# Attention and two MLPs on one core: the first MLP in six tiles of 512 tokens instead of eight of 384

## The chip, the core and the metric

The kernel runs on one core of a Trainium2 chip. The core has a matrix engine (TensorE, PE in the profile, with its weight loads as PEld), a vector engine (VectorE, DVE), an activation engine (ScalarE, ACT), GpSimd (POOL), and SyncE (SP), which here only issues DMA transfers. Each engine runs its own instructions in their order and waits on semaphores for the others. The metric is the device time of one execution in microseconds (us), lower is better.

## What is computed

Three layers in a row, over 4 x 768 = 3072 tokens of 8 heads x 64 = 512 features, in fp32:

```python
for c in range(S // 32):                       # attention in chunks of 32 queries
    k_full = concat([mem_k, k[max(0, 32*c - 16) : 32*c + 40]])      # 8 memory keys and a window
    a = exp(s - max(s));  a = a / (sum(a) + 1e-9)                   # s = q_c @ k_full.T / 8
    out[32*c : 32*c + 32] = a @ v_full
h = x @ w_in;  g = where(h > 0, h, exp(min(h, 0)) - 1);  x = g @ w_out      # first MLP, 512-2048-512
h = x @ w_in2; g = s * relu(h)**2 + b;                   y = g @ w_out2     # second MLP, 512-2048-512
```

## The kernel before

**Attention.** The tokens are cut into 24 units of 128 (U). For a unit u there are three steps: S (step_S: 64 small matmuls of scores on PE, then softmax on DVE, with the exp on ACT; units at the edge of a batch, u % 6 in (0, 5), have a mask added first), P (step_P: the probabilities are transposed into the tile pt), and V (values: 64 small matmuls with pt, then to_x). For the first NU0 = 6 units P is four PE transposes and a copy of their result; for the others it is 16 transposes of 32x32 blocks on DVE, and V of u and S of u+1 share one step (step_VS), V first.

**First MLP.** Each fp32 operand is split into a high and a low part in fp32r, and a product is three matmuls (mm3, L326 to L328). A tile t is a run of units; sizes = [3] * 8, so 384 tokens. The 2048 hidden features are 16 columns c of 128. A slot (t, c) is h1(t, c), 12 matmuls into psH, with the ELU behind it (L350, L351 on ACT, L352 on DVE gives g; gh on ACT and gl on DVE, L184, are its two parts), and out1 of the slot two before it, 12 matmuls into the four accumulators acc. The slots run (0, 0..5), (1, 0..15), (0, 6..15), (2, 0..15), ... (7, 0..15). Since tile 0 is interrupted, its accumulators go out to part_dram and are added back later (L376); at the end of a tile the accumulators are evacuated (big) and stored to y_dram.

**Where attention runs.** Units of tile 0 go before the first slot. Those of tile 1 are spread over slots (0, 0..5), those of tile 2 over (0, 6..15), the others over tiles 2 to TATT - 1 = 4, by a count of steps (beside). From tile 2 on a unit's output goes through DRAM: xs to x_dram (to_x), and load_x reads a whole tile back four slots before its end, copies it to xh on ACT and takes xl on DVE. In slots of tiles 0 and 1 the weights are converted and split (split_w); after the attention, from (5, 0) on, prepare makes the sums of the second MLP's weights and stores them to s_dram.

**Second MLP.** A Strassen-like scheme with seven products (ORDER), in three passes of 1024 tokens; pieces of the weights come from s_dram by a ring of 12 buffers (ws), and load_blocks makes the seven token blocks xc of a pass. Its matmuls have 512 columns.

**What sets the order.** Instructions go out in the order of the program text as a scheduler has moved them (it weighs estimated times and the priorities of the code), each engine in its own queue. Pools give the buffers; before, the first 8 weight columns (NFREE) lay in one pool on the right and the rest in one on the left, whose memory was given back as a whole when MLP one neared its end.

Of the kernel before, what the change touches and what calls it, by code (L numbers as in the profile page):

```python
# [20 lines left out]
P = 128  # L21
# [6 lines left out]
NP = H // 2  # L28
NU0 = 6
HF = 6  # L30
TATT = 5
NFREE = 8
MICRO = 8
HN, NT2 = 512, 3
ORDER = (1, 2, 6, 5, 7, 3, 4)
BANK = {1: 1, 2: 2, 6: 1, 5: 5, 7: 1, 3: 5, 4: 1}
# [17 lines left out]
def tile_attention_then_two_mlps(ctx, tc, q_in, k_in, v_in, w1, w2, s_in, b_in, out):  # L54
# [22 lines left out]
    def engine(step):  # L77
# [4 lines left out]

    sizes = [3] * 8
    assert sum(sizes) == NU
# [6 lines left out]
    mctx = ExitStack()  # L91
    early = [ExitStack(), ExitStack()]
    wps = [early[0].enter_context(tc.tile_pool(name="wpa", bufs=1, side="right")),
           mctx.enter_context(tc.tile_pool(name="wpb", bufs=1))]
    wst = mctx.enter_context(tc.tile_pool(name="wst", bufs=3))
    one = mctx.enter_context(tc.tile_pool(name="one", bufs=1))
    xp = mctx.enter_context(tc.tile_pool(name="xp", bufs=1))
    gp = mctx.enter_context(tc.tile_pool(name="gp", bufs=4))
# [23 lines left out]
    def load_w(w, c, i):  # L122

        r = wps[c >= NFREE].tile([P, DM, 2], I32, tag=f"w{i}_{c}", name=f"raw{i}_{c}")
        nc.sync.dma_start(out=r, in_=w[c, i].bitcast(I32).rearrange("p (n z) -> p n z", z=2))
        return r
# [15 lines left out]
    def split_w(c, i, raw):  # L142

        t = wst.tile([P, DM], I32, tag="t", name="t")
        yield from to_f32(raw, t)
        nm = "io"[i]
        parts = wps[c >= NFREE].tile([P, 2, DM], F32R, tag=f"w{i}_{c}", name=f"w{i}_{c}")
        hi, lo = parts[:, 0], parts[:, 1]
        nc.scalar.activation(out=hi, in_=f(t), func=AF.Copy)
        sub(lo, f(t), hi)  # L150
        W[nm, c], WT[nm, c] = (hi, lo), parts
        yield
# [211 lines left out]
    def put_out(t, c, n):  # L364
# [6 lines left out]
        if c == NF - 1 or c == HF - 1 and split:  # L371
            for m, acc in enumerate(ACC[t]):
                with tc.high_priority(400):
                    if c == NF - 1 and split:
                        o = PART.pop(m)
                        nc.vector.tensor_tensor(out=o, in0=o, in1=acc[:, :n], op=ALU.add)  # L376
                    else:
                        o = big_tile(n, t >= TATT and m > 0 or m == 3 and t >= 2)
                        if m % 2:
                            nc.vector.tensor_copy(o, acc[:, :n])  # L380
                        else:
                            nc.scalar.activation(out=o, in_=acc[:, :n], func=AF.Copy)
                store = nc.scalar if t == NTILE1 - 1 else nc.sync
                store.dma_start(out=y_dram[:, m, t0:t0 + n] if c == NF - 1 else part_dram[:, m, :n], in_=o)
# [138 lines left out]
    pieces = pieces * NT2  # L523
    ws, used = [], [0]

    def load_pieces(n):

        while len(ws) < min(n, len(pieces)):
            lay, ii, jj = pieces[len(ws)]
            w = p2["wsp"].tile([P, 2, 2 * P], F32R, tag="ws", name="ws")  # L530
            nc.sync.dma_start(out=f(w), in_=s_dram[lay, ii, :, PIECE[jj]])
            ws.append(w)
# [8 lines left out]
    XC = {}  # L541

    def load_blocks(t):

        t0 = t * 2 * HN
        xc = XC[t] = {j: p2["xcp"].tile([P, 2, 2, HN], F32R, tag=f"xc{j}", name=f"xc{j}") for j in ORDER}
        b12 = p2["yrp"].tile([P, 2, HN], F32, tag="yr", name="b12")
        b11, b21, b22 = (f(xc[j][:, 1]) for j in (1, 2, 3))
        for o, r, z in ((b11, 0, 0), (b12, 0, 1), (b22, 1, 1), (b21, 1, 0)):
            nc.sync.dma_start(out=o, in_=y_dram[:, 2 * r:2 * r + 2, t0 + z * HN:t0 + (z + 1) * HN])  # L550
        if t == 0:
            load_pieces(12)
        t3, t2, t4 = (p2["yrp"].tile([P, 2, HN], F32, tag="yr", name=nm) for nm in ("t3", "t2", "t4"))
        for o, x, y in ((t3, b22, b12), (b12, b12, b11), (t2, b22, b12), (t4, b21, t2)):
# [3 lines left out]
        for j in ORDER:  # L558
            nc.scalar.activation(out=xc[j][:, 0], in_=src[j], func=AF.Copy)
            sub(xc[j][:, 1], src[j], xc[j][:, 0])  # L560
            yield

    def open_second():

        for nm, k, c in (("xcp", 1, ctx), ("wsp", 12, ctx), ("yrp", 4, early[1])):
            p2[nm] = c.enter_context(tc.tile_pool(name=nm, bufs=k, side="right", reuse_waits="tile"))
        p2["blocks"] = load_blocks(0)

    def mlp1_step(t, c):
# [6 lines left out]
        elif t == 0:  # L576
            a0, total, k, ks = ready[1], ready[2] - ready[1], min(c - HF, NF - HF - 4), NF - HF - 3
        elif 1 < t < TATT:
            a0, total, k, ks = ready[2], len(steps) - ready[2], NF * (t - 2) + c, NF * (TATT - 2)

# [4 lines left out]
        elif t == 1:  # L585
            n0 = 8 * HF + 12
            wt = [(w1, max(n0 + (MICRO * NF - n0) * (2 * c + z) // 28, MICRO * (c + z)), 4) for z in (1, 2)]
        if c == 0 and t == TATT:
            actx.close()
            op.append(mctx.enter_context(tc.tile_pool(name="op2", bufs=2)))  # L590
            p2["prep"] = early[1].enter_context(tc.tile_pool(name="prep", bufs=2, side="right", reuse_waits="tile"))
            p2["steps"] = prepare_all()
            nc.sync.dma_start(out=s_sb, in_=s_in.to_broadcast([P, 1]))
            nc.sync.dma_start(out=b_sb, in_=b_in.to_broadcast([P, 1]))
        if t < 2:
            weights_to(w1, MICRO * (c + 1), 4)
        if t == NTILE1 - 1 and c == NFREE + 2:
            early[1].close()
            early[0].close()
            open_second()  # L600
# [5 lines left out]
        prepared(t, 2 * c + 2)  # L606
        if t == NTILE1 - 1 and c >= NFREE + 2:
            for _ in range(3):
                next(p2["blocks"], None)
# [4 lines left out]
    def prepared(t, n):  # L614

        want = min(NPREP * (2 * NF * (t - TATT) + n) // (2 * NF * (NTILE1 - TATT) - 2 * (NF - NFREE)), NPREP)
        while t >= TATT and p2["n"] < want:
            next(p2["steps"])
# [12 lines left out]
    for slot in seq[-2:]:  # L631
# [5 lines left out]

    early[1].close()
    g2p, evp, outp, p2["yrp"] = (
        ctx.enter_context(tc.tile_pool(name=nm, bufs=k, reuse_waits="tile"))  # L640
        for nm, k in (("g2p", 4), ("evp", 5), ("outp", 4), ("yrp2", 4)))
    ghp = ctx.enter_context(tc.tile_pool(name="ghp", bufs=3, side="right", reuse_waits="tile"))
    psp = ctx.enter_context(tc.tile_pool(name="psp", bufs=8, space=PSUM, reuse_waits="tile"))
# [15 lines left out]
    def first_layer(t, i, g):  # L659

        xc, ii, acc = XC[t], i % 2, {}
        for j in ORDER:
# [4 lines left out]
            for k in range(2):  # L667
                mm3(o, (w[:, 0], w[:, 1]), (xc[j][:, 0], xc[j][:, 1]), lambda a: a[:, k * P:(k + 1) * P],
                    lambda a: a[:, k], j in (1, 2, 5) and k == 0, k == 1, j not in (1, 2, 5))
# [25 lines left out]
    def second_layer(t, gs, beside):  # L695

        keep, acc = {}, {}
        for j in ORDER:
# [4 lines left out]
            for q, g in enumerate(gs):  # L703
                gl, gh = (ghp.tile([P, 2, HN], F32R, tag=nm, name=nm) for nm in ("g2l", "g2h"))
                nc.scalar.activation(out=gh, in_=g[:, block], func=AF.Copy)  # L705
# [98 lines left out]
```

## Time and profile before

| | us |
|---|---|
| median of 3 runs (1089.6 to 1096.9) | 1091.55 |
| the profiled execution | 1094.46 |
| its span, from first to last instruction | 1092.7 |
| first matmul of the first MLP | 28.67 |
| first matmul of the second MLP | 623.38 |
| PE busy in the span | 1072.1 |
| DVE busy | 783.6 |
| ACT busy | 592.1 |

The span is what the trace shows; the run's time has 1.76 us around it. Starts are in us from the span's start. A matmul's duration in the trace overlaps that of the next one, so its price is the distance of starts. "PEclk" is the clock that TensorE was granted, as a share of its full 2.4 GHz. "Idle before" is the time in which an engine had nothing to do in front of a row, with the instruction that ended it.

### The profile page before, as it was taken

To read this page: it belongs to the slowest core of one execution; us is meant where nothing else is said; L and a number is where in the kernel's file an instruction comes from. 1 tells how busy PE (TensorE), PEld (TensorE's weight loads), DVE (VectorE), ACT (ScalarE), POOL (GpSimd) and SP (SyncE) were. 2 spreads that over 40 slices of the span, in tenths; PEclk is the share of its full clock that TensorE was granted. 3 is DMA by queue.
4 is the path that set the end of the run, shared out by engine and by line. 5 is a ranking of instruction groups with operands and counts; after the bars stand their busy time and mean duration, and the time that the engine had idled before them with its cause. 6 is when DMAs were issued, how large, how long until landed. Compare 5 with 4: busy or idle time off the path is not lost.

```text
span 1092.7 us, 20633 instructions
## 1 busy us (share of the span) xinstructions
PE 1072.1 (98%) x8206; PEld 966.0 (88%) x8206; DVE 783.6 (72%) x1299; ACT 592.1 (54%) x939; POOL 0.7 (0%) x6
## 2 busy tenths in 40 slices
PE   7999999999999999999999999999999999999998
PEld 5889999999999999999999987788888788888887
DVE  6899846778678777998884655697356696365854
ACT  4888444334434446787784455754355644255542
POOL 0000000000000000000000000000000000000000
PEclk7899999999999999999999999999999999999999
DMA  8955032433524315898886266777766777766673
GB/s 307 373 221 220 1 109 88 153 102 105 174 81 145 125 40 173 319 335 298 331 326 236 90 187 191 244 210 231 230 191 185 231 214 225 212 197 191 200 204 127
DMA packets 98113, 213.70 MB, mean 196 GB/s; under 512 B 9952, under 2 KB 27360, under 8 KB 95968
## 3 DMA queue, kind: packets, MB, share of 16 engines
q1 hardware_dynamic: 97440, 211.59, 59.4%
q8 instruction: 65, 1.06, 0.4%
q10 hardware_dynamic: 576, 0.79, 0.2%
q14 instruction: 32, 0.26, 0.1%
HBM read 164.89 MB, written 47.45 MB: 194 GB/s over the span
## 4 chain that ended last, share of the span: by engine, by line
PE 82%; DVE 8%; DMA 5%; ACT 3%; issue 1%; SPq 0%; ACTq 0%; DVEq 0%
PE psH L326 14%; PE psH L328 13%; PE psH L327 13%; PE psL L327 7%; PE acc L326 6%; PE psL L328 6%; PE acc L327 6%; PE acc L328 6%; PE psL L326 6%; DVE pt L258 2%; DMA xc<-y_dram 2%; DMA xl<-x_dram 1%; DMA x_dram<-xs 1%; PE psVS L278 1%; PE psVS L219 1%
## 5 line engine op out<-in xcount | busy, mean ns | idle before, releaser
L326 PE MATMUL psH<-xh,w 128*128 128x384 f32 x512 | 175.4, 343 | 2.6 <-ACT pt L180 1.1
L326 PE MATMUL acc<-gh,w 128*128 128x384 f32 x512 | 173.0, 339 | 0.9 <-DVE big L376 0.8
L328 PE MATMUL psH<-xh,w 128*128 128x384 f32 x512 | 173.6, 339 | 0.0
L327 PE MATMUL psH<-xl,w 128*128 128x384 f32 x512 | 173.2, 338 | 0.2 <-DVE xl L184 0.2
L327 PE MATMUL acc<-gl,w 128*128 128x384 f32 x512 | 171.9, 336 | 0.0
L328 PE MATMUL acc<-gh,w 128*128 128x384 f32 x512 | 171.9, 336 | 0.0
L705 ACT ACTIVATE g2h<-g 128x1024 fp32r<-128x1024 f32 x84 | 89.2, 1062 | 89.9 <-PE psL L328 89.6
L327 PE MATMUL psL<-g2l,ws 128*128 128x512 f32 x336 | 131.0, 390 | 1.6 <-DVE g2l L184 1.6
L326 PE MATMUL psH<-xc,ws 128*128 128x512 f32 x336 | 131.8, 397 | 0.6 <-ACT p L656 0.6
L328 PE MATMUL psH<-xc,ws 128*128 128x512 f32 x336 | 131.1, 390 | 0.0
L326 PE MATMUL psL<-g2h,ws 128*128 128x512 f32 x336 | 130.4, 389 | 0.6 <-ACT g2h L705 0.6
L327 PE MATMUL psH<-xc,ws 128*128 128x512 f32 x336 | 130.9, 390 | 0.0
L328 PE MATMUL psL<-g2h,ws 128*128 128x512 f32 x336 | 130.7, 389 | 0.0
L184 DVE TENSOR_TENSOR g2l<-g,g2h 128x1024 fp32r<-128x1024 f32 x84 | 102.2, 1222 | 39.5 <-ACT g2h L705 39.2
L350 ACT ACTIVATE g<-psH 128x384 f32<-128x384 f32 x128 | 62.5, 488 | 113.1 <-PE psH L328 67.0
L180 ACT ACTIVATE gh<-g 128x384 fp32r<-128x384 f32 x128 | 66.9, 522 | 86.8 <-DVE g L352 85.6
L352 DVE SCALAR_TENSOR_TENSOR g<-g,psH 128x384 f32<-128x384 f32 x128 | 70.5, 551 | 49.3 <-ACT g L351 48.4
L326 PEld LDWEIGHTS psH<-xh,w 128*128 128x128 f32 x512 | 97.0, 189 | 5.2 <-ACT pt L180 1.4
L326 PEld LDWEIGHTS acc<-gh,w 128*128 128x128 f32 x512 | 96.6, 189 | 2.4 <-DVE big L376 1.1
L327 PEld LDWEIGHTS psH<-xl,w 128*128 128x128 f32 x512 | 97.1, 190 | 0.5 <-DVE xl L184 0.4
L328 PEld LDWEIGHTS psH<-xh,w 128*128 128x128 f32 x512 | 97.2, 190 | 0.2
L327 PEld LDWEIGHTS acc<-gl,w 128*128 128x128 f32 x512 | 96.2, 188 | 0.3 <-DVE gl L184 0.2
(97 smaller groups left out, 1668.1 us busy)
## 6 DMA issues: line engine op xcount, KB each, us to landing
ws<-s_dram SPq DMA_DIRECT2D x336, 256.0 KB, 2.9
raw<-w SPq DMA_DIRECT2D x64, 512.0 KB, 5.4
s_dram<-right SPq DMA_DIRECT2D x16, 1024.0 KB, 4.5
kb<-k SPq DMA_DIRECT2D x24, 512.0 KB, 5.6
v<-v SPq DMA_DIRECT2D x24, 512.0 KB, 4.3
s_dram<-left SPq DMA_DIRECT2D x16, 768.0 KB, 3.6
q<-q SPq DMA_DIRECT2D x24, 256.0 KB, 5.5
out<-r SPq DMA_DIRECT2D x24, 256.0 KB, 3.5
```

The source lines that it names most:

```text
L180: return nc.scalar.activation(out=hi, in_=src, func=AF.Copy)
L184: return nc.vector.tensor_tensor(out=lo, in0=src, in1=f(hi), op=ALU.subtract)
L219: mm = nc.tensor.matmul(ps[o, z, r * NCK:(r + 1) * NCK], q[rows, r * U + c * CH:r * U + (c + 1) * CH], kb[rows, r, c * NCK:(c + 1) * NCK], ...
L258: nc.vector.transpose(out=pt[k * CH:(k + 1) * CH, :, rows], in_=sm[rows, :, z, n0:n0 + CH])
L278: nc.tensor.matmul(ps[r % 2 * D:(r % 2 + 1) * D, z, o:o + CH], v[rows, (r * NC + c) * D:(r * NC + c + 1) * D], pt[rows, r, cs], start=True ...
L326: nc.tensor.matmul(o, sa(a[0]), sb(b[0]), start=first, stop=False, skip_group_check=again)
L327: nc.tensor.matmul(o, sa(a[0]), sb(b[1]), start=False, stop=False, skip_group_check=again)
L328: return nc.tensor.matmul(o, sa(a[1]), sb(b[0]), start=False, stop=last, skip_group_check=again)
L350: nc.scalar.activation(out=g[:, :n], in_=ps[:, :n], func=AF.Relu, scale=-1.0)
L352: nc.vector.scalar_tensor_tensor(out=g[:, :n], in0=g[:, :n], scalar=-1.0, in1=ps[:, :n], op0=ALU.add, op1=ALU.max)
L705: nc.scalar.activation(out=gh, in_=g[:, block], func=AF.Copy)
```

## The change

The first MLP takes tiles of four units, 512 tokens, six of them. Units 0 to 3 (tile 0) go before the first slot and units 4 to 7 beside slots (0, 0..5); NU0 = 8, so the first eight units are transposed on PE. The other attention units, from 12 on, are spread over the slots from (2, 0) to ATT_END = (3, 8) instead of over three tiles, and prepare starts at (3, 8). The weights of the first layer lie in one pool (wpi), with the x tiles on the same side; those of the second in another (wpo). The second MLP takes its buffers over from these pools one by one, under the same tags: the blocks xc and the ring of pieces from weight columns w0_c (two pieces to a buffer) and from an x tile, the first blocks yr from w1_0 to w1_3, and the parts of g for its second layer from the other x tile. The order of the operations within the second MLP is not edited.

```diff
-NU0 = 6
+NU0 = 8
-TATT = 5
-NFREE = 8
+ATT_END = (3, 8)
+NBLOCK = 10
...
-    sizes = [3] * 8
+    sizes = [4] * 6
...
-    early = [ExitStack(), ExitStack()]
-    wps = [early[0].enter_context(tc.tile_pool(name="wpa", bufs=1, side="right")),
-           mctx.enter_context(tc.tile_pool(name="wpb", bufs=1))]
+    wps = [ctx.enter_context(tc.tile_pool(name="wpi", bufs=1, side="right")),
+           mctx.enter_context(tc.tile_pool(name="wpo", bufs=1))]
-    xp = mctx.enter_context(tc.tile_pool(name="xp", bufs=1))
+    xp = ctx.enter_context(tc.tile_pool(name="xp", bufs=1, side="right"))
...
-        r = wps[c >= NFREE].tile([P, DM, 2], I32, tag=f"w{i}_{c}", name=f"raw{i}_{c}")
+        r = wps[i].tile([P, DM, 2], I32, tag=f"w{i}_{c}", name=f"raw{i}_{c}")
...
+            n = len(ws) % 12
+            if len(ws) < 12 and n % 2 == 0:
+                p2["ws"] += [high(10 + n // 2)]
+            w = p2["ws"][n // 2].rearrange("p z (j n) -> p (z j) n", j=2)[:, 2 * (n % 2):2 * (n % 2) + 2]
...
+    def high(c):
+        return wps[0].tile([P, 2, HN], F32R, tag=f"w0_{c}", name=f"hi{c}")
...
-        elif 1 < t < TATT:
-            a0, total, k, ks = ready[2], len(steps) - ready[2], NF * (t - 2) + c, NF * (TATT - 2)
+        elif t > 1 and (t, c) < ATT_END:
+            a0, total, k, ks = ready[2], len(steps) - ready[2], NF * (t - 2) + c, NF * (ATT_END[0] - 2) + ATT_END[1]
...
-        if t == NTILE1 - 1 and c == NFREE + 2:
-            early[1].close()
-            early[0].close()
+        if t == NTILE1 - 1 and c == NBLOCK:
             open_second()
...
+        begin = 2 * (NF * ATT_END[0] + ATT_END[1])
+        want = min(NPREP * (2 * NF * t + n - begin) // (2 * NF * (NTILE1 - 1) + 2 * NBLOCK - 2 - begin), NPREP)
```

How PE's instructions stand at the start, before (psS scores, psP transposes, psV values, psH the first layer-one matmuls; the scheduler's counts of small matmuls are those of its own rows):

```order
L219 MATMUL psS<-kb,q 32x64 x15
L251 MATMUL psP<-ident,sm_103 128x128 x4
L278 MATMUL psV<-pt,v 64x32 x32
L219 MATMUL psS<-kb,q 32x64 x32
L326 MATMUL psH<-xh,w_0_382 128x384
```

And now, from the same scores on:

```order
L218 MATMUL psS<-kb,q 32x64 x15
L250 MATMUL psP<-ident,sm_103 128x128 x4
L277 MATMUL psV<-pt,v 64x32 x32
L218 MATMUL psS<-kb,q 32x64 x32
L250 MATMUL psP<-ident,sm_104 128x128 x4
L277 MATMUL psV<-pt,v 64x32 x32
L218 MATMUL psS<-kb,q 32x64 x32
L325 MATMUL psH<-xh,w_0_433 128x512
```

The transposes, the values and the following scores of unit 3 have moved ahead of the first psH matmul.

On DVE, before, the end of unit 15's probabilities (multiply by the reciprocal sums, 16 transposes into pt) and what stands until the softmax of unit 16 begins (nmx), with the xl of an x tile:

```order
L237 TENSOR_TENSOR sm_103<-sm_103,rs 128x2x4x64
L258 STREAM_TRANSPOSE pt<-sm_103 32x4x32
L352 SCALAR_TENSOR_TENSOR g<-g,psH 128x384
L258 STREAM_TRANSPOSE pt<-sm_103 32x4x32 x4
L184 TENSOR_TENSOR gl<-g,gh 128x384
L258 STREAM_TRANSPOSE pt<-sm_103 32x4x32 x11
L184 TENSOR_TENSOR xl<-xl,xh 128x1536
L352 SCALAR_TENSOR_TENSOR g<-g,psH 128x384
L184 TENSOR_TENSOR gl<-g,gh 128x384
L352 SCALAR_TENSOR_TENSOR g<-g,psH 128x384
L184 TENSOR_TENSOR gl<-g,gh 128x384
L231 TENSOR_REDUCE nmx<-psVS 128x8
```

Now the like place, the end of unit 16's and the begin of unit 17's, which has a mask (cmask):

```order
L236 TENSOR_TENSOR sm_103<-sm_103,rs 128x2x4x64
L257 STREAM_TRANSPOSE pt<-sm_103 32x4x32 x11
L351 SCALAR_TENSOR_TENSOR g<-g,psH 128x512
L257 STREAM_TRANSPOSE pt<-sm_103 32x4x32 x4
L183 TENSOR_TENSOR gl<-g,gh 128x512
L257 STREAM_TRANSPOSE pt<-sm_103 32x4x32
L183 TENSOR_TENSOR xl<-xl,xh 128x2048
L351 SCALAR_TENSOR_TENSOR g<-g,psH 128x512
L227 TENSOR_TENSOR sm_104<-psVS,cmask_93 128x2x4x64
L183 TENSOR_TENSOR gl<-g,gh 128x512
L230 TENSOR_REDUCE nmx<-sm_104 128x8
```

Between xl and the next softmax stand one g and one gl now, not two of each; on PE, 48 matmuls stand between the scores of one unit and the values of the next from unit 13 on (60 at the turn of a tile), where 72 or 84 stood before.

## Rows read from the trace of the kernel before

**Rows 1.** The page: span.

```profile
span 1092.7 us, 20633 instructions
PE 1072.1 (98%) x8206; PEld 966.0 (88%) x8206; DVE 783.6 (72%) x1299; ACT 592.1 (54%) x939; POOL 0.7 (0%) x6
```

**Rows 2.** Windows by stage: stretch, length, busy time of each engine, PEclk, DMA share.

```profile
0.00:28.67 28.67, 21.47 (x546) 16.71 (x546) 18.06 (x38) 12.35 (x20) 0.70 (x6) 0.78 0.84 311
28.67:96.86 68.19, 63.76 (x730) 57.25 (x725) 65.08 (x128) 61.57 (x120) 0.00 (x0) 0.94 0.81 309
96.86:623.38 526.52, 524.21 (x4921) 516.33 (x4921) 403.21 (x851) 287.01 (x538) 0.00 (x0) 1.00 0.48 166
623.38:1092.70 469.32, 462.67 (x2017) 375.70 (x2016) 297.27 (x284) 231.20 (x264) 0.00 (x0) 1.00 0.70 205
```

**Rows 3.** Timeline of PE: first matmuls of slots (5, 0) and (7, 15).

```profile
419.04 0.44 PE L326 MATMUL psH<-xh,w 128*128 128x384 f32 x1
...
615.07 0.33 PE L326 MATMUL psH<-xh,w 128*128 128x384 f32 x1
```

**Rows 4.** Timeline of PE: two matmuls of the second MLP, 202 apart.

```profile
880.18 0.39 PE L326 MATMUL psL<-g2h,ws 128*128 128x512 f32 x1
...
925.97 0.39 PE L327 MATMUL psL<-g2l,ws 128*128 128x512 f32 x1
```

**Rows 5.** Timeline of PE, then DVE: start, duration, what; values, scores, first psH.

```profile
16.87 1.94 PE L278 MATMUL psV<-pt,v 64*64 64x32 f32 x64
...
22.76 1.11 PE L251 MATMUL psP<-ident,sm 128*128 128x128 f32 x4
24.62 1.72 PE L278 MATMUL psV<-pt,v 64*64 64x32 f32 x56 [0.75 <-ACT pt L180]
27.19 0.44 PE L278 MATMUL psV<-pt,v 64*64 64x32 f32 x8 [0.85 <-issue]
27.56 1.18 PE L219 MATMUL psS<-kb,q 64*32 64x64 f32 x64
28.67 0.69 PE L326 MATMUL psH<-xh,w 128*128 128x384 f32 x1
...
30.32 0.68 DVE L237 TENSOR_TENSOR sm<-sm,rs 128x512 f32<-128x512 f32 x1
```

**Rows 6.** Timeline of PE at unit 6's values, then windows behind them.

```profile
74.74 0.30 PE L278 MATMUL psVS<-pt,v 64*64 64x32 f32 x2 [0.93 <-DVE pt L258]
75.40 0.78 PE L278 MATMUL psVS<-pt,v 64*64 64x32 f32 x38 [0.36 <-DVE pt L258]
...
77.00:81.00 4.00, 4.00 (x16) 3.87 (x14) 4.00 (x9) 3.47 (x8) 0.00 (x0) 0.57 0.97 334
```

**Rows 7.** Timeline of PE and DVE: unit 15, scores, first and last transposes, values.

```profile
275.25 0.86 PE L219 MATMUL psVS<-kb,q 64*32 64x64 f32 x64
...
284.74 2.58 DVE L258 STREAM_TRANSPOSE pt<-sm 32x128 f32<-32x128 f32 x8
...
290.82 0.38 PE L278 MATMUL psVS<-pt,v 64*64 64x32 f32 x12
```

**Rows 8.** Timeline of PE: values of unit 16.

```profile
305.40 0.55 PE L278 MATMUL psVS<-pt,v 64*64 64x32 f32 x24
306.43 0.30 PE L278 MATMUL psVS<-pt,v 64*64 64x32 f32 x2 [0.48 <-DVE pt L258]
307.09 0.78 PE L278 MATMUL psVS<-pt,v 64*64 64x32 f32 x38 [0.36 <-DVE pt L258]
```

**Rows 9.** Groups by line and form: busy time, mean ns, idle before; 384 and 512 columns.

```profile
L352 DVE SCALAR_TENSOR_TENSOR g<-g,psH 128x384 f32<-128x384 f32 x128 | 70.5, 551 | 49.3 <-ACT g L351 48.4
L649 DVE TENSOR_TENSOR g<-m,psH 128x512 f32<-128x512 f32 x24 | 16.5, 687 | 24.1 <-PE psH L328 18.2 <-ACT m L656 5.6
```

**Rows 10.** Timeline: x tile 2 on its way through DRAM.

```profile
168.12 0.60 ACT L180 ACTIVATE xs<-psVS 128x512 f32<-128x512 f32 x1 [0.51 <-PE psVS L219]
...
180.64 1.76 DVE L184 TENSOR_TENSOR xl<-xl,xh 128x1536 fp32r<-128x1536 f32 x1 [1.00 <-ACT xh L302]
```

**Rows 11.** The page: DMA issues, us from issue to landing.

```profile
ws<-s_dram SPq DMA_DIRECT2D x336, 256.0 KB, 2.9
```

## What the change does to the time

> **What bounds the kernel now.** I read the span first: PE is busy 98% of 1092.7 us [rows 1]. The stage windows then say where it is not: 7.2 us before the first layer-one matmul at 28.67, 4.4 us up to 96.86, only 2.3 us from there to the second MLP at 623.38, 6.7 us in the second MLP [rows 2]. So the time is a count of matmuls times their spacing, plus the attention's own small matmuls, plus few waits. The profiled execution took 1094.46 us, 1.76 more than its span; the median is 0.27% under it. My sum goes by the span; the result is scaled by 1091.55/1094.46.
>
> **Spacing of a matmul.** From 419.04 to 615.07 there is no idle, and 47 slots of 24 matmuls, 1128, start in 196.03 us: 173.8 ns for 384 columns [rows 3]. In the second MLP 202 spacings of 512-column matmuls fill 880.18 to 925.97: 226.7 ns [rows 4]. So a third more columns costs 30.4% more, as if about 14.8 ns of each matmul were fixed.
>
> **The change, part by part.**
>
> *Fewer, wider matmuls.* MLP one has 128 slots of 24 = 3072 matmuls before and 96 of 24 = 2304 after: 3072 x 0.1738 = 533.9 us against 2304 x 0.22667 = 522.2 us: **-11.7**, if the fp32r matmul of MLP one keeps the pace of that of MLP two, whose form is the same but for the tiles' names. By a price per column (0.1738 x 512/384 = 0.2317) it is 533.9 us again: 0. I take -11.7, since a 512-column row is nearest to a 512-column matmul. The Trainium skill ("TensorE: Matmul & The Clock Gate", section "Back-to-back issue gap") gives a warm gap of about N/2.4 + 2.5 ns, 162.5 and 215.8 ns here: by it the gain is an estimated 2.0 us and not 11.7. The trace shows 11 ns more than that at either width, so the measurement decides.
>
> *Longer start.* A first tile of four units puts P3, V3 and S5 of unit 3 ahead of the first layer-one matmul. Before, DVE ends unit 3's softmax at 30.32 + 0.68 = 31.0 [rows 5]. Behind it come four transposes at half clock (1.1, as those of unit 2 at 22.76), the pt copy's wait (0.75, as at 24.62), V3 (1.7) and most of S5 (0.8): 35.3 against 28.67, **+6.6**. Bounds: V ends of units 0 and 2 lie 8.8 us apart, 4.4 a unit; with V2's extra 0.85 us of issue, 7.5.
>
> *The stretch from there to slot (1,6).* 264 matmuls: 45.9 us of 68.19 before, 59.8 after. Of the other 22.3 us before, about 10.7 are PE work of units 3 to 6, 4.4 idle, 1.8 the half clock at its head (twelve matmuls 0.32 us apart). After, PE work is that of units 4 to 7, four times 2.85 = 11.4. Unit 6 was turned by DVE's 32x32 transposes, and PE waited 0.93 + 0.36 us inside its V; from 77 to 81 us the clock then stood at 0.57, which costs 4 x 0.43 = 1.7 [rows 6]. Both go, as units 6 and 7 are now transposed on PE. Of the rest I take 6.2 us: the floor is 59.8 + 11.4 + 1.8 = 73.0, and with all 22.3 it is 82.2. DVE (65.1 us busy of 68.2) and ACT (61.6) get some 7% more nominal work in the longer stretch, so they do not pass PE. I say 77.5, **+9.3**.
>
> *From slot (1,6) to the second MLP.* Before, 526.52 us: 2808 matmuls (115 slots and 48) 488.0, 17 units with V and S the other 38.5, that is 2.27 each, of which 2.75 us in all were waits, so 2.1 each without. After: 83 slots of 5.440 and 48 matmuls, 462.4; 16 units 33.6; together 496.0.
>
> *The waits in V.* Here the change bites. For each of these units DVE does, behind the scores S on PE, maximum, subtract, (ACT's exp), sum, reciprocal, multiply and 16 transposes of 0.30, and V of the unit waits for the last. Unit 15 is typical: S ends at 275.25 + 0.86 = 276.11, the transposes at 284.74 + 2.58 = 287.32: 11.2 us with one g and one gl between; PE came to V at 290.82, having 84 matmuls [rows 7]. Unit 16, with 72, waited 1.33 us in V (two idles, 0.48 and 0.36, and pieces) [rows 8]. After, the attention has 24 slots for twelve units from (2,0) on, and the order has 48 matmuls between S and the next V: 10.9 us, some 11.4 until V's last matmuls need the last transposes. The chain becomes 11.2 + 2 x 0.13 (g and gl at 0.69 and not 0.55 [rows 9]) = 11.5. So:
> - plain units (15, 16, 19, 20, 22): 0.2 each, 1.0; unit 14 0.4;
> - 9, 10, 11 and 13, with evacuations and partial adds of the accumulators, a mask, or a V that stands 12 matmuls earlier: 1.6, 1.9, 1.35, 1.9;
> - 23, masked: 0.9; units 8, 12 and 18 have 60 matmuls or more: 0;
> - 17 and 21, where xl of the next x tile stands in DVE ahead of the softmax. Before, that chain took 14.3 us from xs at 168.12 to the end of xl at 180.64 + 1.76 [rows 10]; for 2048 columns ACT takes 0.6 and DVE 0.55 more and the transfer is a third larger: 16.6 to 17.8. S of the next unit ends 13.0 us on, so DVE starts its softmax some 4 us late: 5.1 (with mask, g and gl) and 3.8.
>
> Sum 17.9 against 2.75 before. 496.0 + 17.9 = 513.9: **-12.6**. Bounds: 2.75 (they hide as before) and 30 (each of the seven waits above 0.9 us brings a half clock at 1.7 us, as from 77 to 81; unit 16's 1.33 brought none).
>
> *x staging.* X2 is ready 17.8 us behind V11 at the latest, PE has 19 us of work until h1(2,0). Without that cover: up to 4 us.
>
> *Weights in parts, buffers taken over singly.* In the second MLP the instructions keep their order. Its first twelve pieces wait each for h1 of the last six slots and land 2.9 us after issue [rows 11]; 36 matmuls (8.2 us) lie between the last h1 and the first use. 0, with +/-1.5 for the block loads. Without that cover, 2.9 us once. prepare runs in 34 slots of 5.44 = 185 us instead of 40 of 4.17 = 167: no wait on PE before, none after.
>
> Sum: +6.6 + 9.3 - 12.6 = **+3.3 us** on 1092.7, i.e. 1096.0; with 1.76 and scaled 1095.
>
> **Rivals.** About 1% (10.9 us) is what a measurement tells from no change: faster is under 1080.6, slower over 1102.5.
> 1. *The waits hide.* If the evacuations, the partial adds and xl run in gaps of DVE and not, as I have them, ahead of a softmax, and the plain chains stay 0.2 us under unit 15's, the waits stay at 2.75 and the sum is 3.3 - 15.1 = -11.8: 1080. For it: DVE is busy 77% of the long stretch [rows 2], and of 17 units only four waited before. Against: their gap was 72 to 84 matmuls, 12.5 to 14.6 us, and DVE does its queue in order.
> 2. *Waits and clock.* As forecast, but each long wait also drops the clock to its lower level (1.2 GHz) for some us: +12, 1107. It decides from a wait of about 1 us on. For it: after 0.93 us at 74.7 the clock fell. Against: after the pair of unit 16 it did not; that wait at 74.7 stood in a stretch with other idles.
> 3. *No gain per matmul.* If the spacing goes by columns (231.6 ns) the term of -11.7 is 0: 1107. For it: the weights and moving operands now lie apart, which no row here prices. Against: the two spacings differ by less than the columns do [rows 3, 4]. By the formula of the Trainium skill ("TensorE: Matmul & The Clock Gate", "Back-to-back issue gap") the estimate is 1104; no row here bears it out at either width.
>
> **How the numbers follow.** Forecast 0.54 (1083 to 1102 by its own bounds: start -2 to +1, stretch +/-4.5, waits 10 to 22), rival 1 0.20, rival 2 0.17, rival 3 0.09. Predicted is the forecast, 1095. Rival 1 stands on the edge of "faster": with the start and the stretch at their low ends it is under it; I give it 0.16 faster and 0.04 within. Rivals 2 and 3 are mostly slower: 0.21 of their 0.26, 0.05 within. So faster 0.16, same 0.63, slower 0.21. The range 1080 to 1107 leaves out about 0.2.
>
> **What would show it.** 226.7 ns between 512-column matmuls of psH and acc; h1(0,0) at 35 us (under 33 or over 37: wrong); slot (1,6) at 112.8; the second MLP's first matmul at about 626.7; idle of PE before psVS released by DVE's pt, 15 to 18 us in sum, largest at units 17 and 21, with xl in front of the softmax; the granted clock at 1.00 after them (else rival 2). I am wrong if the V waits sum to under 6 us, if the second MLP changes by over 2 us, or if the first tiles are bounded by DVE or DMA, for which the share is 0.84 at the start.

## The result and the profile after

| | before | after |
|---|---|---|
| median of 7 runs each (us) | 1092.85 | 1099.35 |
| profiled execution, span (us) | 1092.7 | 1097.1 |
| first matmul of the first MLP | 28.67 | 35.29 |
| first matmul of slot (1, 6) | 96.86 | 109.96 |
| first matmul of the second MLP | 623.38 | 628.58 |

The ratio is 1.007, with an interval of 1.0052 to 1.0087: 0.7% slower, inside the 1% that the prediction called "no change", and inside its range. The span grew by 4.4 us where 3.3 were forecast.

The windows by stage of the changed kernel (stretch, length, busy time of PE, PEld, DVE, ACT, POOL, then granted clock, DMA share, GB/s) answer to [rows 2]:

```profile
0.00:35.29 35.29, 25.50 (x678) 20.08 (x678) 24.68 (x52) 16.34 (x27) 0.70 (x6) 0.72 0.86 322
35.29:109.96 74.67, 73.41 (x734) 58.05 (x730) 70.87 (x132) 67.38 (x125) 0.00 (x0) 0.97 0.76 276
109.96:628.58 518.62, 509.74 (x4026) 414.32 (x4025) 375.15 (x733) 262.98 (x426) 0.00 (x0) 0.99 0.47 163
628.58:1097.10 468.52, 462.54 (x2017) 375.63 (x2015) 297.38 (x284) 231.06 (x264) 0.00 (x0) 1.00 0.71 206
```

Against before the stages changed by +6.6, +6.5, -7.9 and -0.8 us. The long third stage is where the gain was to be: PE now idles 8.9 us in it, not 2.3.

**The spacing.** The timeline of PE of the changed kernel, first matmuls of slots (4, 0) and (5, 14), answers to [rows 3]:

```profile
446.92 0.39 PE L325 MATMUL psH<-xh,w 128*128 128x512 f32 x1
...
612.12 0.39 PE L325 MATMUL psH<-xh,w 128*128 128x512 f32 x1
```

30 slots of 24 matmuls in 165.20 us are 229.4 ns each, without any idle, not the 226.7 of [rows 4]. Looked at singly, the gaps are not even: every group of 12 (a switch from psH to acc or back) begins with gaps of some 230, 224, 231, 236, 228, 232, 231 ns (those of acc without the 224 and the second 231), then runs at 226.7, and its last gap is 235. The same pattern comes in every slot.

**The waits.** The changed kernel's summary of the tile psVS says what ended PE's idle time before its matmuls (releaser: us in sum, times):

```profile
its engine sat idle before it (us, times) until:
  DVE pt L257: 15.9, 39
  PE psVS L218: 8.0, 10
```

The first line is the wait for the transposes (of weight loads and matmuls both). Measured on the matmuls alone, as the time from V's first to its last start over the 0.92 us of an undisturbed V, it is 14.4 us over the units 8 to 23 (0.8 of it are a few matmuls of MLP one that stand between the two parts of V of units 10 and 13). The longest but one is unit 17; here its rows, DVE first, then PE:

```profile
299.56 2.29 DVE L183 TENSOR_TENSOR xl<-xl,xh 128x2048 fp32r<-128x2048 f32 x1 [0.88 <-ACT xh L301]
301.77 0.68 DVE L351 SCALAR_TENSOR_TENSOR g<-g,psH 128x512 f32<-128x512 f32 x1
302.36 0.69 DVE L227 TENSOR_TENSOR sm<-psVS,cmask 128x512 f32<-128x512 f32 x1
...
312.44 1.93 DVE L257 STREAM_TRANSPOSE pt<-sm 32x128 f32<-32x128 f32 x6
```

```profile
311.45 0.59 PE L277 MATMUL psVS<-pt,v 64*64 64x32 f32 x18
313.12 0.31 PE L277 MATMUL psVS<-pt,v 64*64 64x32 f32 x6 [1.08 <-DVE pt L257]
313.77 0.30 PE L277 MATMUL psVS<-pt,v 64*64 64x32 f32 x2 [0.34 <-DVE pt L257]
314.43 0.78 PE L277 MATMUL psVS<-pt,v 64*64 64x32 f32 x38 [0.36 <-DVE pt L257]
```

xl stands ahead of the mask as the order showed, the transposes end at 314.37, and V goes in pieces behind them. The windows show what followed that wait, and unit 21's (3.2 us, from 370.65 on):

```profile
316.00:320.00 4.00, 4.00 (x11) 3.16 (x12) 3.06 (x5) 1.23 (x2) 0.00 (x0) 0.57 0.95 285
...
372.00:376.00 4.00, 2.95 (x112) 2.46 (x112) 3.07 (x8) 0.63 (x1) 0.00 (x0) 0.75 0.00 0
376.00:380.00 4.00, 4.00 (x25) 3.22 (x15) 2.39 (x5) 1.40 (x3) 0.00 (x0) 0.82 0.68 201
```

The granted clock fell to its lower level (1.2 GHz) for some 3.5 us each time: 4 x 0.43 = 1.7 us lost, and 4 x 0.25 + 4 x 0.18 = 1.7 again.

So the third stage adds up: 2040 matmuls x 0.2294 = 468.0, 15 units x 2.05 (V and S without waits, as unit 19) and V of unit 23, 1.3, = 32.0, waits in V 13.6 (14.4 without the matmuls of MLP one inside), a wait of 2.1 for the accumulators of tile 0 at 252.9, clock 2.8 (of the 3.4, some 0.6 lie inside unit 21's V): 518.5, measured 518.6.

Two questions were left for the experiments: what makes a 512-column matmul dearer here than in the second MLP, and whether the waits are indeed a matter of how densely the attention stands.

### The profile page after: what moved, and what is told of

Same layout as the page of the kernel before. It is cut to its first block, busy times and chain, and to the rows that moved or that the text cites. A ratio compares the mean times of both kernels' runs of the same rounds, so it can differ in the third digit from the quotient of the medians.

```text
span 1097.1 us, 18801 instructions
## 1 busy us (share of the span) xinstructions
PE 1071.2 (98%) x7446; PEld 868.1 (79%) x7446; DVE 768.1 (70%) x1199; ACT 577.7 (53%) x839; POOL 0.7 (0%) x6
## 4 chain that ended last, share of the span: by engine, by line
PE 78%; DVE 11%; DMA 5%; ACT 3%; issue 1%; SPq 0%; DVEq 0%; ACTq 0%
PE psH L325 13%; PE psH L327 13%; PE psH L326 12%; PE psL L326 7%; PE psL L327 6%; PE psL L325 6%; PE acc L325 6%; PE acc L326 6%; PE acc L327 6%; DVE pt L257 4%; DMA hi<-y_dram 2%; DMA xl<-x_dram 1%; DMA x_dram<-xs 1%; PE psVS L277 1%; PE psV L277 1%
## 5 line engine op out<-in xcount | busy, mean ns | idle before, releaser
L325 PE MATMUL acc<-gh,w 128*128 128x512 f32 x384 | 152.4, 397 | 2.6 <-DVE big L375 1.9
L325 PE MATMUL psH<-xh,w 128*128 128x512 f32 x384 | 153.1, 399 | 0.2 <-DVE g L351 0.2
L327 PE MATMUL psH<-xh,w 128*128 128x512 f32 x384 | 151.6, 395 | 0.0
L326 PE MATMUL acc<-gl,w 128*128 128x512 f32 x384 | 151.5, 395 | 0.0
L327 PE MATMUL acc<-gh,w 128*128 128x512 f32 x384 | 150.8, 393 | 0.0
L326 PE MATMUL psH<-xl,w 128*128 128x512 f32 x384 | 150.6, 392 | 0.0
L351 DVE SCALAR_TENSOR_TENSOR g<-g,psH 128x512 f32<-128x512 f32 x96 | 65.8, 685 | 72.8 <-ACT g L350 72.2
L179 ACT ACTIVATE gh<-g 128x512 fp32r<-128x512 f32 x96 | 60.6, 631 | 79.4 <-DVE g L351 78.7
L325 PE MATMUL psH<-hi,hi 128*128 128x512 f32 x240 | 93.8, 397 | 0.4 <-ACT p L673 0.3
L327 PE MATMUL psH<-hi,hi 128*128 128x512 f32 x240 | 93.7, 391 | 0.0
L326 PE MATMUL psH<-hi,hi 128*128 128x512 f32 x240 | 93.6, 390 | 0.0
L326 PE MATMUL psL<-g2l,hi 128*128 128x512 f32 x224 | 87.4, 390 | 1.8 <-DVE g2l L183 1.8
L327 PE MATMUL psL<-g2xl,hi 128*128 128x512 f32 x224 | 87.1, 389 | 0.0
L325 PE MATMUL psL<-g2xl,hi 128*128 128x512 f32 x224 | 86.8, 389 | 0.0
L326 PEld LDWEIGHTS psH<-xl,w 128*128 128x128 f32 x384 | 72.7, 189 | 16.6 <-DVE xl L183 0.4
L183 DVE TENSOR_TENSOR gl<-g,gh 128x512 fp32r<-128x512 f32 x96 | 66.3, 690 | 26.6 <-ACT gh L179 25.7
```

The source lines that it names most:

```text
L179: return nc.scalar.activation(out=hi, in_=src, func=AF.Copy)
L183: return nc.vector.tensor_tensor(out=lo, in0=src, in1=f(hi), op=ALU.subtract)
L325: nc.tensor.matmul(o, sa(a[0]), sb(b[0]), start=first, stop=False, skip_group_check=again)
L326: nc.tensor.matmul(o, sa(a[0]), sb(b[1]), start=False, stop=False, skip_group_check=again)
L327: return nc.tensor.matmul(o, sa(a[1]), sb(b[0]), start=False, stop=last, skip_group_check=again)
L351: nc.vector.scalar_tensor_tensor(out=g[:, :n], in0=g[:, :n], scalar=-1.0, in1=ps[:, :n], op0=ALU.add, op1=ALU.max)
```

## First four runs: place of the operands, and density of the attention

Three theories for the spacing: the moving operands change their part of memory with each group (x above 128 KB, gh and gl below); the weights do (w_in above, w_out below); or it is the width alone. In the first run the x tiles go to the other side, in the second the weights are split by column as before.

```diff
-    xp = ctx.enter_context(tc.tile_pool(name="xp", bufs=1, side="right"))
+    xp = ctx.enter_context(tc.tile_pool(name="xp", bufs=1))      # ahead of wps
```

> The changed kernel with only the x tiles moved: from 128 to 160 KB of each partition down to 2 to 34 KB, so that the moving operands of both layers (x, then gh and gl) lie below 128 KB, while the weights of layer one stay above (160 to 224 KB) and those of layer two below. Theory 'the moving operand's change of part costs': the spacing of MLP-one matmuls falls from 229.5 to 226.7 ns, 2304 x 2.8 = 6.4 us less, about 1093 us. Theory 'the weights' change of part costs': the uneven gaps (up to 236 ns) stay at least where the weights go from above to below, at the start of each group of 12 matmuls into acc; spacing 228 to 229.5, 0 to 3 us less. Theory 'it is the width of 512 alone': 229.5 as now, no change.

Measured: 1111.03 us, ratio to before 1.0166 (1.0139 to 1.0192). No theory had this. The timeline of PE, first matmul of an acc group, of the psH group behind it, and of the next acc group:

```profile
455.23 0.39 PE L325 MATMUL acc<-gh,w 128*128 128x512 f32 x1
...
457.96 0.39 PE L325 MATMUL psH<-xh,w 128*128 128x512 f32 x1
...
460.76 0.39 PE L325 MATMUL acc<-gh,w 128*128 128x512 f32 x1
```

12 matmuls of psH now take 2.80 us, 233 ns each, with gaps of 232 and 235 in turn all through the group, while those of acc take 2.73, 228 each. The second MLP, which takes two of its xc and four parts of g from these x tiles, became 7 us longer too. So it is not a matter of switching alone: a combination of weights and moving operand is dear as long as it lasts. The spacing is not the whole of the time, though. The span (1110.1) is 13.0 us longer: the second MLP by 6.9, the third stage by 8.6, while the first two are 2.4 shorter. Of the 8.6, 230.3 ns instead of 229.4 make 1.7. The rest goes with the waits and the lower clock behind them: 11.9 us of clock in sum (what is missing to the full clock, added up over the profile in pieces of 4 us) where the changed kernel lost 3.4, some of it inside the waits.

```diff
-        r = wps[i].tile(...)            parts = wps[i].tile(...)
+        r = wps[c >= 8].tile(...)       parts = wps[c >= 8].tile(...)
-        return wps[0].tile([P, 2, HN], F32R, tag=f"w0_{c}", name=f"hi{c}")
+        return wps[0].tile([P, 2, HN], F32R, tag=f"w{c // 8}_{c % 8}", name=f"hi{c}")
```

(yr takes w0_8, w0_9, w0_10 and w1_8 then.)

> The changed kernel with only the weights' places changed back to a split by column (columns 0 to 7 of both layers above 128 KB, 8 to 15 below), as the kernel before has it; the x tiles stay above and gh, gl below. Weights then change part some 6 times per tile and not 32 times. Theory 'weights': spacing near 227 ns, about 6 us less, 1093 us. Theory 'moving operand': 229.5 stays, 1099 us. Theory 'width': 229.5 stays.

Measured: 1101.94 us (1.0066 to 1.0107 of before). Neither of the two places: 231.4 ns between slots (4, 0) and (5, 14). About half of the groups are at 233 ns: psH for the columns from 8 on, whose weights are on the left and x on the right, and acc for those below 8, with weights on the right and gh, gl on the left. The others are at 229 to 230. In both runs the dear groups are those with weights and moving operand on different sides. But the second MLP contradicts "part of memory": in the changed kernel two of its three gl buffers lie at 120 to 128 KB and its weights above 160 KB, and its matmuls stand 226.7 ns apart. What these gl buffers share with the weights is the pool side, and with it something smaller: the pools on the right end 32 bytes short of a multiple of 64, so all operands of these matmuls there leave 32 modulo 64 (w0_0 at 163808, x at 131040), and all on the left leave 0 (w1_0 at 2240, gh at 75968). That became the next theory.

The third run is the other question. It only spreads the attention more thinly, into slots of tile 1 in which DVE is busy 27.8 us of 55.1 in the changed kernel:

```diff
-    "pt": ("a", "a", "-", "a", "v"),
-    "xh": ("a", "a", "-", "a", "a"),
+    "pt": ("a", "a", "a", "a", "v"),
+    "xh": ("a", "a", "a", "a", "a"),
...
-        elif t == 0:
-            a0, total, k, ks = ready[1], ready[2] - ready[1], min(c - HF, NF - HF - 4), NF - HF - 3
-        elif t > 1 and (t, c) < ATT_END:
-            a0, total, k, ks = ready[2], len(steps) - ready[2], NF * (t - 2) + c, NF * (ATT_END[0] - 2) + ATT_END[1]
+        elif (t, c) < ATT_END and (t != 1 or c >= HF):
+            k = c - HF if t == 1 else NF - HF + c - HF if t == 0 else 2 * (NF - HF) + NF * (t - 2) + c
+            a0, total, ks = ready[1], len(steps) - ready[1], 2 * (NF - HF) + NF * (ATT_END[0] - 2) + ATT_END[1]
```

(The first lines name the engine of two copies, ACT as elsewhere, for the slots of tile 1, where no attention stood before.)

> The changed kernel with one thing else: attention units 8 to 23 are spread over 44 slots from (1, 6) to (3, 8) instead of units 8 to 11 over (0, 6..12) and 12 to 23 over (2, 0) to (3, 8), so some 66 matmuls (15 us) stand between scores and values and not 48 (11 us). Theory 'the attention is too dense': the waits in V, 14.4 us in sum in the changed kernel, fall under 3 us and the two stretches at a lower clock (1.7 us each) vanish: 14 to 17 us less, about 1083 us. Rival 'DVE is the bound there': slots (1, 6) to (1, 15) grow by over 5 us in sum, and the total falls by less than 7 us.

Measured: 1084.17 us, 0.9927 of before (0.9907 to 0.9947), 15 us under the changed kernel. The summary of psVS, as above for the changed kernel, has no line with DVE pt any more:

```profile
its engine sat idle before it (us, times) until:
  PE psVS L218: 8.0, 5
  ACT xs L179: 7.6, 5
  issue: 5.0, 14
  ACT gh L179: 0.4, 1
```

The sum of the waits in V is 0, both stretches of lower clock at 316 and 372 are gone, and the third stage is 503.5 us (518.6). With 60 to 72 matmuls between scores and values the chain fits. The rival, DVE as the bound, fell: the slots (1, 6) to (1, 15) grew from 55.1 to 63.3 us, but by the attention's own PE work moved there (four V and S of 2.1 us), not by waits.

The fourth run is the changed kernel's memory with the tiles of before.

```diff
-NU0 = 8
+NU0 = 6
-ATT_END = (3, 8)
+ATT_END = (5, 0)
-    sizes = [4] * 6
+    sizes = [3] * 8
```

> The changed kernel's memory layout with the tiles of before: eight tiles of 384 tokens, six units transposed on PE, attention until (5, 0). Theory 'a change of part costs': every group of 12 matmuls begins with gaps such as 185, 176, 182 ns that the kernel before shows only in 5 groups of each tile (22 ns each); with 256 groups up to 5 us more than before, about 1097 us. Theory 'width': the gaps stay flat at 173 to 174 ns, 1093 us. The start and the waits in V are as before in both.

Measured: 1096.15 us, 1.0037 of before (1.0024 to 1.005). The place costs at 384 columns too, but less: each group begins with gaps of 173, 175, 178, 185, 176, 182 ns and then runs at 173.4. Before, only five groups in each tile do so, those whose weights have just gone from right to left (the way back costs nothing there); and there the groups with weights on the right and x on the left run at 173.4 throughout. So at 384 columns a lasting difference of sides costs nothing, a change some 20 to 30 ns; at 512 both cost. The head of such a group before, slot (5, 8):

```profile
452.48 0.35 PE L326 MATMUL psH<-xh,w 128*128 128x384 f32 x1
452.67 0.34 PE L327 MATMUL psH<-xl,w 128*128 128x384 f32 x1
```

## Next four runs: 32 bytes

```diff
+    pad = const.tile([P, 8], F32, name="pad")
+    nc.vector.memset(pad, 0.0)
     s_sb = const.tile([P, 1], F32, name="s_sb")
```

This tile is used by nothing. It shifts everything on the left by 32 bytes, so that all tiles leave 32 modulo 64, and changes no part of memory.

> The changed kernel with one unused 32-byte tile more (and its memset) in the first pool on the left, so that everything on the left starts 32 bytes higher: all pools on the left then stand at addresses that leave 32 modulo 64, as those on the right do already; the parts of memory stay as in the changed kernel. Theory 'the address modulo 64 counts, not the part': weights and moving operand no longer differ between or within groups, gaps are flat and the spacing in MLP one falls from 229.4 to 226.7 ns; 2304 x 2.8 = 6.4 us less, about 1092 to 1093 us. Theory 'the part of memory (above or below 128 KB) counts': 229.4 and the uneven first gaps of each group of 12 stay, 1099 us.

Measured: 1095.06 us, 1.0033 of before (1.0016 to 1.005), 4.3 less than the changed kernel. Timeline of PE: first matmul of a psH group and of the acc group behind it:

```profile
449.26 0.39 PE L327 MATMUL psH<-xh,w 128*128 128x512 f32 x1
...
451.98 0.39 PE L327 MATMUL acc<-gh,w 128*128 128x512 f32 x1
```

2.72 us, 226.7 ns each, and all gaps of these groups are 226 or 227: the pattern is gone. Of the 6.4 us that this is worth, 4.5 show in the span (1092.6): the waits in V sum to 16.5 us, not 14.4, and the lower clock costs 5.1 us, not 3.4. Unit 17 alone waits 5.1 us, not 2.6. ACT's row of the x tile in front of it, in the changed kernel:

```profile
297.62 1.91 ACT L301 ACTIVATE xh<-xl 128x2048 fp32r<-128x2048 f32 x1 [0.66 <-DMA xl<-x_dram]
```

The same row in this run:

```profile
295.43 1.92 ACT L303 ACTIVATE xh<-xl 128x2048 fp32r<-128x2048 f32 x1 [2.61 <-DMA xl<-x_dram]
```

The read of the tile took 5.3 us in the changed kernel and landed 0.2 us ahead of unit 16's V (297.75); here it took 6.7 and landed 1.9 us behind it (293.52). The first run, with 230.3 ns between matmuls, had it 1.7 us behind and waited 4.9. So the wait went with the landing of the tile and not with the spacing; why the read took longer is open.

The same tile was then added to the run with the x tiles on the left (this one), to the kernel before, and to the early attention (the next two).

> The x tiles at the low end of memory (in the run before with them there, the matmuls of layer one were 232.9 ns apart all through, with gaps of 232 and 235 in turn) and the 32 bytes. Weights of layer one lie above 128 KB, x below, both at 32 modulo 64. Theory 'modulo 64': 226.7 ns, and 1111 us falls by 2304 x 3 to 4 ns = 7 to 9 us and more. Theory 'part': 232.9 ns stay, 1111 us.

Measured: 1095.75 us (1111.03 without the pad; 1.0022 to 1.0063 of before). Weights above 160 KB, x below 35 KB, and the psH group is as fast as in the run above (226.7 ns, slots (4, 0) to (5, 14) in 163.2 us). First matmul of a psH group and of the acc group behind it:

```profile
449.70 0.39 PE L327 MATMUL psH<-xh,w 128*128 128x512 f32 x1
...
452.42 0.39 PE L327 MATMUL acc<-gh,w 128*128 128x512 f32 x1
```

This settles it: not the part of memory, but whether the two addresses leave the same remainder modulo 64. (Wherever they did here they also agreed modulo 128 and 256, so that the runs do not tell these apart; modulo 32 they agreed everywhere.) Of the 18.6 us less in the span than without the pad, the second MLP has 7.7 and the spacing of MLP one about 8.

> The kernel before with the 32 bytes. Theory 'modulo 64': the groups that begin with 185, 176, 182 ns (two into acc and three into psH in each tile) become flat at 173 to 174, 22 ns each over 40 groups: about 1 us less, 1091 us, hardly measurable in time but plain in the gaps. Theory 'part': the gaps stay.

Measured: 1089.84 us, 0.9991 of before (0.9975 to 1.0007): no difference in time that can be told, as expected for 1 us. In the gaps it is plain: no group between 420 and 619 us begins with 185 ns any more, where 15 did.

> The early attention (units 8 to 23 from slot (1, 6) on) and the 32 bytes together. Theory 'modulo 64': 1084 less 6.4, about 1078 us, no waits in V. Theory 'part': as the early attention alone, 1084 us.

Measured: 1081.44 us, 0.9904 of before (0.9884 to 0.9924), 2.7 under the early attention alone and not 6.4. The spacing is 226.7 ns and V waits for nothing, but two other waits, with the lower clock behind one, cost 3.6 us more than under the early attention alone. The first stood there before: the last of the four adds that free tile 0's accumulators for the next tile, DVE at 256.02. It cost PE 2.1 us in the changed kernel and 2.2 under the early attention alone; now it costs 2.7, and the lower clock follows, 1.7:

```profile
256.02 0.69 DVE L377 TENSOR_TENSOR big<-big,acc 128x512 f32<-128x512 f32 x1 [1.33 <-issue]
```

```profile
258.00:262.00 4.00, 4.00 (x12) 3.14 (x12) 2.97 (x8) 2.95 (x3) 0.00 (x0) 0.59 0.16 61
```

The second, 1.4 us at 531, is the evacuation of tile 4 behind prepare's work on ACT and DVE. It did not come again in the runs below.

## Last four runs: what the faster matmuls run into

All four stand on the run just shown; the second to fourth keep the edit of the first. The four partial sums of tile 0 are read back into a ring of three buffers, so the fourth waits until the first has been added and stored.

```diff
-                PART[m] = big_tile(n)
+                PART[m] = big_tile(n, m == 3)
```

> Early attention and the 32 bytes, and the fourth of tile 0's partial sums read back into a spare buffer (wst) instead of the ring of three, so that its transfer need not wait for the first one's store. In the run without this PE waited 2.9 us at 253.9 for the last of the four adds (DVE itself idle 1.3 us ahead of it) and then had the lower clock for some 3 us. Theory 'the ring of three is the cause': that wait and the lower clock go, 4 to 5 us less, about 1077 us. Rival 'the add stands behind the softmax in DVE's queue anyway': under 2 us less, 1080 to 1081 us.

Measured: 1082.57 us, 0.9902 of before (0.9887 to 0.9918): no gain over the run without it. The wait itself went, as the theory has it (the four adds run in one piece from 247.3), and the second MLP starts at 607.6 and not 611.9. It gave the time back there: PE waited 3.0 us at 611.3, and the lower clock behind it cost 1.7. Timeline of ACT, then the window behind it:

```profile
607.23 1.67 ACTq L385 DMA_DIRECT2D y_dram<-big  x3
613.83 0.60 ACT L674 ACTIVATE m<-psH 128x512 f32<-128x512 f32 x1 [6.07 <-DMA y_dram<-big]
```

```profile
614.00:618.00 4.00, 3.52 (x11) 2.82 (x12) 0.69 (x1) 1.51 (x3) 0.00 (x0) 0.73 0.18 45
```

The first result that the second MLP sets aside (m) takes the memory of a wst buffer. One more use of that ring had turned it by one place, so that this buffer now held the last of the last tile's four sums, whose store landed at 613.75.

The next has the pad on the other side, the one after it an earlier end of the attention:

```diff
-    pad = const.tile([P, 8], F32, name="pad")
-    nc.vector.memset(pad, 0.0)
+    padp = ctx.enter_context(tc.tile_pool(name="padp", bufs=1, side="right"))      # ahead of wps
+    nc.vector.memset(padp.tile([P, 8], F32, name="pad"), 0.0)
```

> The same with the 32 unused bytes at the right end of memory instead of the left: everything then stands at 0 modulo 64. Theory 'weights and moving operands need the same remainder modulo 64': 226.7 ns and the time of the run beside it. Rival 'the remainder must be 32': the spacing is above 226.7 everywhere, 2304 and more matmuls, over 5 us more.

Measured: 1081.13 us, 0.9893 of before (0.9875 to 0.991), and 226.7 ns: the remainder may be 0 or 32, weights and moving operand need the same one. The wait at the head of the second MLP is the same as in the run before.

```diff
-ATT_END = (3, 8)
+ATT_END = (3, 4)
```

> The same as the first of these with the attention's end four slots earlier, at (3, 4): 40 slots for 16 units, 60 matmuls (13.6 us) between scores and values, against a chain of 11.5 us. Theory of the prediction (waits come where the chain passes the gap): still no waits in V except where an xl stands ahead of a softmax, there up to 2 us; prepare gets four slots more, so that the wait for the accumulators at 531 us (1.9 us) goes: within 2 us of the first. Rival 'density matters well before that': waits over 4 us in sum, 3 us and more slower.

Measured: 1085.24 us, 0.9928 (0.9911 to 0.9945). With 60 matmuls between scores and values V waits 2.8 us in all (unit 9 2.1, unit 23 0.8), against 1.0 in the first of the three, and the one at the head of the second MLP is 4.7 us, against 3.0. The profiled spans of the two differ by 4.0 us: 1.9 of waits in V, 1.7 of lower clock behind unit 9's, 1.7 at that head, less 1.3 for a wait for accumulators at 188.3 that is gone. The medians, 2.7 apart, lie between the two forecasts. The theory was not quite met: units 9 and 23 wait without an xl ahead of their softmax (in DVE's queue stand splits of the weights in unit 9's chain, and two evacuations in unit 23's). That density costs anything beyond the chain was not shown.

In the last run the attention ends at (3, 8) again, and two pools of the second MLP change places.

```diff
-    g2p, evp, outp, yrp, ghp = (
+    g2p, outp, evp, yrp, ghp = (
...
-        for nm, k, side in (("g2p", 4, "left"), ("evp", 5, "left"), ("outp", 4, "left"), ("yrp", 1, "left"),
+        for nm, k, side in (("g2p", 4, "left"), ("outp", 4, "left"), ("evp", 5, "left"), ("yrp", 1, "left"),
```

> The run with the fourth partial sum in a spare buffer, and in the second MLP the pools evp and outp in the other order, so that the first set-aside result (m) takes memory that the g parts held and not the buffers (wst) from which the last tile's sums are still on their way to y_dram. In the run without this ACT waited 6.1 us for that store, PE 3.2 us at 611.3, and the clock was lower for some 5 us behind it. Theory 'the buffer taken over too early is the cause': both go, 4 to 5 us less, about 1078 us. Rival 'the blocks or pieces are late there as well': PE still idles 2 us and more at the head of the second MLP, 1081 to 1083 us.

Measured: 1076.00 us, 0.9848 of before (0.9825 to 0.9872), 6.6 under the run without it and faster than both kernels. (1.5 of the 6.6 are between the two measurements of the kernel before; the profiled spans differ by 5.5, of which 4.3 are in the second MLP.) The wait of 3.0 and the lower clock behind it are gone. The same rows of ACT:

```profile
606.05 1.67 ACTq L385 DMA_DIRECT2D y_dram<-big  x3
608.03 0.60 ACT L674 ACTIVATE m<-psH 128x512 f32<-128x512 f32 x1 [1.44 <-DMA y_dram<-big]
```

and its windows by stage:

```profile
0.00:36.30 36.30, 27.19 (x680) 21.34 (x681) 25.48 (x54) 17.10 (x28) 0.70 (x6) 0.68 0.86 316
36.30:108.93 72.63, 71.16 (x729) 56.72 (x727) 70.24 (x131) 66.50 (x123) 0.00 (x0) 0.99 0.78 282
108.93:606.90 497.97, 496.40 (x4027) 409.07 (x4026) 373.24 (x734) 262.14 (x427) 0.00 (x0) 1.00 0.49 170
606.90:1074.70 467.80, 461.35 (x2015) 375.36 (x2013) 296.90 (x284) 230.44 (x263) 0.00 (x0) 1.00 0.71 206
```

The third stage (cut 0.4 us into the second MLP, whose first matmul is at 606.47) is 497.5 us, 1.5 more than the 496.0 that the prediction had for this stage without its waits. Unit 17 still waits 1.0 in V, and PE 1.2 for accumulators at 187.1.

## Why the prediction was right, and which of its steps were not

- **Start, +6.6.** Right: 35.29 where 35.3 was said. That it fits to 0.1 us is luck: in the other runs with six tiles, where the steps of the start are the same, it lies between 34.1 and 37.2.
- **To slot (1, 6), +9.3.** Measured +6.5: 74.67, not 77.5. The floor of 73.0 was right but for 0.7 of spacing; of the 4.5 us that 77.5 puts on top of it for waits and hand-overs 1.7 were there. PE idles only 1.3 us in it.
- **Fewer, wider matmuls, -11.7.** Wrong, by 6.4 us. The step that failed is "I take -11.7, since a 512-column row is nearest": the row was of the second MLP, where all operands stand at the same remainder modulo 64, and the price was taken to belong to the shape alone. In MLP one it is 229.4, 2304 x 0.2294 = 528.6, -5.3. The third rival had the place of the operands as its cause but priced it by columns (231.7); no row priced it, as was said. The traces of before did hold a sign of it, the 185, 176, 182 ns at the head of five groups in each tile, which the even mean of [rows 3] hides. With the 32 bytes the term is as forecast (226.7). (The "14.8 ns of each matmul" that seemed fixed are 15.1 by its own two spacings; nothing rests on it.) By the formula in the Trainium skill ("TensorE: Matmul & The Clock Gate", section "Back-to-back issue gap"), which is given there for a single matmul on its own, the gap would be an estimated 215.8 ns; the trace shows 11 ns more even where the gaps are flat.
- **The waits in V, 17.9.** Mechanism right, shown by the run with the attention spread more thinly; the size 14.4. Unit by unit, forecast and measured: 9 1.6 and 1.5, 10 1.9 and 2.6, 11 1.35 and 1.0, 13 1.9 and 1.6, 14 0.4 and 0.1, 17 5.1 and 2.6, 21 3.8 and 3.2, 23 0.9 and 0.7; the plain ones 15 and 16 0.6, 19, 20 and 22 0 (0.2 each said). (Without the matmuls of MLP one inside, unit 10 has 2.0 and unit 13 1.3.) The term that was furthest off is unit 17's x tile: from xs at 287.30 to the end of xl at 301.85 are 14.6 us, not 16.6 to 17.8. With the 32 bytes they were 16.5 and the wait 5.1.
- **Accumulators of tile 0.** The forecast had the adds only as a part of the waits in V; 2.1 us of PE's wait for them came on top.
- **Clock.** The forecast left it out; two waits, of 2.6 and 3.2 us, brought the lower level for 1.7 us each, as priced for the second rival. Those of 1.0 to 1.6 us brought none, and neither did unit 10's 2.0 and the 2.1 for the accumulators, so "from about 1 us on" was too early. Nor does the length of the wait alone decide: in the first run unit 9's 1.8 us brought it.
- **Second MLP, 0 +/- 1.5.** -0.8. The wait of ACT for the last stores is 1.77 us where before had 2.10, and costs PE nothing.
- **Scaling.** Span +4.4; the medians differ by 6.5, the rest is the spread of runs about their profiled one.

The forecast was close because errors offset each other. In the third stage they are +5.6 for the spacing, +2.8 for the clock and +2.1 for the accumulators against -4.3 in the waits and -1.6 in the units (32.0 and not 33.6), together +4.6; the second stage has -2.8 and the second MLP -0.8. That it landed in the range does not make the matmul term good.

## What to carry to other kernels

Take a matmul's price from one with the same shape and the same placing of both operands, and look at its gaps one by one before a mean is taken. When PE gets faster in a stage, work out anew every chain that hid behind it (here softmax and transposes against 48 matmuls, then the accumulators, then the buffers at the seam): each gave back several us until it was moved. Work that other engines must finish in time belongs where those engines are idle, even if it is wanted much later.

## What the hardware showed that was not expected

An undisturbed stream of fp32r matmuls of 512 columns ran at 226.7 ns when the addresses of weights and moving operand left the same remainder modulo 64 (both 32, or both 0), at 233 ns when one left 0 and the other 32, and at 229.4 when both changed their remainder every 12 matmuls. At 384 columns the lasting difference cost nothing (173.4), a change some 20 to 30 ns in the next group. The same uneven gaps also come in short rows in the second MLP, where all operands leave the same remainder, some of them right behind a gap of 270 to 500 ns in which PE was held up (from 846 and from 857 us in the changed kernel): such gaps show that the stream was disturbed, not by what. Whether it is the remainder modulo 64, 128 or 256, and what shifts of less than 32 bytes would do, was not tried, nor what in the engine causes it.
